# A gated mix of windowed attention and a spatial-gating MLP: row 0's mask by GpSimd fills, softmax maximum and sum by one reduce each, joined last folds, wo scaled one step later, and a PSUM bank of its own for the last 128 output columns

## The chip, the cores and the metric

The kernel runs on one core of a Trainium2 chip. The time is what one execution takes on the device, in microseconds (us). Before the change the median of three runs is 693.05 us (692.97 to 693.73). One further execution was recorded by the hardware profiler; all views of the profile come from it.

A core has five engines that run side by side and wait for each other by semaphores: TensorE (PE, matrix products into PSUM; PEld is its weight load), VectorE (DVE), ScalarE (ACT), GpSimd (POOL) and SyncE (SP, which here only issues DMAs). Each engine takes its instructions in the order in which the program emits them. PSUM has eight banks of 512 fp32 columns on 128 partitions.

## The reference

With S = 2048 rows and D = 1024, cut to what is computed:

```
g   = sigmoid((x * gate_w).sum(-1))                 # one gate per row
a   = attention(x)                                  # 32 heads of 32
        q, k, v = x @ wqkv
        row s attends to rows s, s-2, ..., s-14      # W = 8, dilation 2; negative rows masked
        logits = q . k / sqrt(32); softmax over 8; o = sum of v
        a = o @ wo
b   = gMLP(x)                                       # F = 3584, Fh = 1792
        z = gelu(x @ w_in); z1, z2 = halves; z2 = layernorm(z2)
        b = (z1 * (w_sp @ z2 + b_sp)) @ w_out
out = g * a + (1 - g) * b
```

## The kernel before

All matrix products run on TensorE in one unbroken order: z2's first columns (16 row tiles, L279 to L319), the q, k and v projections in six chunks of 16 tiles (L500 to L519), the rest of z2 (L524), z1 (L576, 14 column tiles of four matmul groups), the two halves of the spatial product as `g_chunk(0)` and `g_chunk(1)` (L593), seven `seven_products` (L701, a Strassen-like scheme for the other half), and last the output products: `mix_pair(0)` (gMLP, rows 0 and 1 of 16 row tiles), `attn_pair(0)` (attention times wo for the same rows) and `both_pairs(q)` for q = 1 to 7.

**Attention** runs on VectorE beside these, for eight groups of four heads. A partition holds 16 consecutive rows. `qk_steps(jh)` (L328) does eight of the 16 rows at a time: one product of q with eight shifted copies of k into `prod`, 8192 elements, then five folds along the head's 32 columns: sums of halves of 16, 8, 4 and 2 columns (all L335, written back into `prod`, where one head's 32 columns take 64 bytes) and the last into the fp32 logits `att_L` (L338). `soft_a` (L342) adds a mask tile, takes the maximum over the window by three halvings and subtracts it; `soft_exp` is one exp on ScalarE; `soft_b` (L352) sums by three halvings, takes the reciprocal and multiplies. `pv_steps(g, jh)` multiplies by v and folds. The logits are laid out as half, window position, row and head, so the eight window positions of one row and head lie 128 bytes apart.

**The order** of the attention's steps between the TensorE work is set by a planner, `Beat` (L220). It keeps a clock of TensorE's columns and one of VectorE; each step comes with a due cost (`4.4`, `2.3` and so on), and after each group of matmuls the planner emits every step that would start within 3 us, and every action whose time (`beat.at`) has come. The costs only set the order of emission. In `attention_steps` (L390) of group g: the folds, `soft_a`, then the two `pv_steps` of group g-1 while exp runs, then `soft_b`. q and k of group g+1 are loaded 1 us (planned) after the folds, v after the `pv_steps`; all these loads and the projections' stores share SP's queue.

**Powers of two.** `whole_power` (L538) finds a scale in steps that are placed apart: a maximum on VectorE, a transpose on TensorE and a reduction on VectorE (L547, L548), a broadcast matmul on TensorE (L550) and the rest on VectorE. For w_out's scale the last two are placed 12 and 24 us after the start of `g_chunk(0)` (L1042). `g_chunk` evacuates each tile on ScalarE (L603), and VectorE adds the bias (L606) and multiplies by z1 (L607), which was stored to DRAM and is loaded back by L460.

**The output.** `mix_pair` (L821) makes seven groups of seven matmuls; the last accumulates into the bank `pb` once VectorE has read it (L842), and the sixth group is read by L844. `wo_scale` (L849) is one VectorE instruction over all of wo in SBUF, which every matmul of `attn_pair` (L893) reads. In `both_pairs` (L905), for the last pair, the last product goes by 384 and 128 columns into one bank, `apb`; each part is combined on VectorE (L883) and stored by SP.

**The mask** tile (L104 to L111) is zero but for row 0's partition, filled with -1e30 where a row has no row to attend to; GpSimd makes it at the start.

Of the kernel before, what the change touches and what calls it, by code (L numbers as in the profile page):

```python
# [15 lines left out]
P = 128  # L16
# [5 lines left out]
HG = 4  # L22
NG = NH // HG
C = HG * DH
W = 8
# [32 lines left out]
def kernel(  # L58
# [42 lines left out]

    ident = sm.tile([P, P], BF, name="ident")
    make_identity(nc, ident[:])
    mask = sm.tile([P, 2 * W * 8 * HG], BF, name="mask")  # L104
    nc.gpsimd.memset(mask[:], 0.0)
    m5 = mask[:].rearrange("p (a w j h) -> p a w j h", a=2, w=W, j=8, h=HG)
    for jh in range(2):
        for w in range(W):
            n = min(8, max(0, 14 - 2 * w - 8 * jh))
            if n > 0:  # L110
                nc.gpsimd.memset(m5[0:1, jh, w, 0:n, :], NEG)  # L111
    zeros = sm.tile([P, NG, 16], BF, name="zeros")
    nc.gpsimd.memset(zeros[:], 0.0)
    g_s = sm.tile([P, 16], F32, name="g_s")
# [30 lines left out]
    v_up = sm.tile([P, 1], I32, name="v_up")  # L145
    back = sm.tile([P, 1], I32, name="back")
    att_L = sm.tile([P, 2 * W * 8 * HG], F32, name="att_L")
    att_m = sm.tile([P, 2, 4, 32], F32, name="att_m")
    att_r = sm.tile([P, 2, 1, 32], F32, name="att_r")
    att_A = sm.tile([P, 2 * W * 8 * HG], BF, name="att_A")  # L150

# [173 lines left out]
    p3 = prod.rearrange("p (w n) -> p w n", w=W)  # L325
    TT = nc.vector.tensor_tensor

    def qk_steps(jh):  # L328
        def mul():
            in0 = _sub_ap(q_t, (8 * jh) * C, [[0, W], [C, 8], [1, C]])  # L330
            in1 = _sub_ap(k_t, (8 * jh) * C, [[2 * C, W], [C, 8], [1, C]])
            TT(prod.rearrange("p (w j c) -> p w j c", w=W, j=8, c=C), in0, in1, ALU.mult)  # L332

        def fold(half):
            return lambda: TT(pv[:, :, 0:half], pv[:, :, 0:half], pv[:, :, half:2 * half], ALU.add)  # L335

        def last():
            TT(L[:, jh * 256:(jh + 1) * 256], pv[:, :, 0], pv[:, :, 1], ALU.add)  # L338

        return [(4.4, mul), (2.3, fold(16)), (1.2, fold(8)), (0.7, fold(4)), (0.6, fold(2)), (0.6, last)]  # L340

    def soft_a():  # L342
        TT(L[:], L[:], mask[:], ALU.add)
        TT(att_m[:], L4[:, :, 0:4, :], L4[:, :, 4:8, :], ALU.max)
        TT(att_m[:, :, 0:2, :], att_m[:, :, 0:2, :], att_m[:, :, 2:4, :], ALU.max)
        TT(att_m[:, :, 0:1, :], att_m[:, :, 0:1, :], att_m[:, :, 1:2, :], ALU.max)
        TT(L4, L4, att_m[:, :, 0:1, :].to_broadcast([P, 2, W, 32]), ALU.subtract)

    def soft_exp():
        nc.scalar.activation(L[:], L[:], ACT.Exp, scale=float(SCALE))  # L350

    def soft_b():  # L352
        TT(att_m[:], L4[:, :, 0:4, :], L4[:, :, 4:8, :], ALU.add)
        TT(att_m[:, :, 0:2, :], att_m[:, :, 0:2, :], att_m[:, :, 2:4, :], ALU.add)
        TT(att_m[:, :, 0:1, :], att_m[:, :, 0:1, :], att_m[:, :, 1:2, :], ALU.add)
        nc.vector.reciprocal(att_r[:], att_m[:, :, 0:1, :])
        TT(A4, L4, att_r[:].to_broadcast([P, 2, W, 32]), ALU.mult)

    def pv_steps(g, jh):
        o_out = obuf[:, :, (g % 2) * C:(g % 2 + 1) * C]  # L360

        def mul():
            in0 = _sub_ap(v_t, (8 * jh) * C, [[2 * C, W], [C, 8], [HG, DH], [1, HG]])
            in1 = _sub_ap(att_A, jh * 256, [[32, W], [HG, 8], [0, DH], [1, HG]])
            TT(prod.rearrange("p (w j d h) -> p w j d h", w=W, j=8, d=DH, h=HG), in0, in1, ALU.mult)  # L365

        def last():
            TT(o_out[:, 8 * jh:8 * jh + 8, :], p3[:, 0, :].rearrange("p (j c) -> p j c", c=C),
               p3[:, 1, :].rearrange("p (j c) -> p j c", c=C), ALU.add)

        return [(4.4, mul), (2.3, lambda: TT(p3[:, 0:4, :], p3[:, 0:4, :], p3[:, 4:8, :], ALU.add)),  # L371
                (1.2, lambda: TT(p3[:, 0:2, :], p3[:, 0:2, :], p3[:, 2:4, :], ALU.add)), (0.7, last)]
# [17 lines left out]
    def attention_steps(t):  # L390
        beat.at(t - 8.0, lambda: load_qk(0))
        beat.at(t + 35.0, lambda: load_v(0))
        for g in range(NG):
            for took, fn in qk_steps(0) + qk_steps(1):
                yield t, took, fn
            t = beat.vector
            if g + 1 < NG:
                beat.at(t + 1.0, lambda g=g: load_qk(g + 1))
            yield t, 2.4, soft_a
            t = beat.vector  # L400
            beat.at(t + (1.0 if g == 0 else 5.0), soft_exp)
            if g == 0:
                t += 5.0
            else:
                for took, fn in pv_steps(g - 1, 0) + pv_steps(g - 1, 1):
                    yield t, took, fn
                t = beat.vector
                if g + 1 < NG:
                    beat.at(t + 1.0, lambda g=g: load_v(g))
                else:  # L410
                    load_v(g)
                if g % 2 == 0:
                    beat.at(t + 1.5, lambda g=g: store_o(g - 1))
            yield t, 2.3, soft_b
            t = beat.vector
        for took, fn in pv_steps(NG - 1, 0) + pv_steps(NG - 1, 1):
            yield t + 5.0, took, fn
        t = beat.vector
        beat.at(t + 14.0, lambda: store_o(NG - 1))
# [398 lines left out]
    def mix_slot(a, n0):  # L818
        return mix_slots[2 * (a % 4) + n0 // 512]
# [85 lines left out]
    def both_pairs(q):  # L905
        a, b = 2 * q, 2 * q + 1
        s, so = row_pair_sums[q % 2], o_sums[q % 2]
        og = [omg[:, r:r + 1] for r in (a, b)]
        ga = [g_s[:, r:r + 1] for r in (a, b)]
        b11, b12, b21, b22 = wo_tiles()  # L910
        a11, a12, a21, a22 = [oT_slots[r % 4][:, 4 * h:4 * h + 4, :] for r in (a, b) for h in range(2)]
        stt = nc.vector.scalar_tensor_tensor
        act = nc.scalar.activation
        wt = [lambda j, k=k: w_t(f_of(q, j), k) for k in range(4)]
        mpa, apa = bank(), bank()
        product7(mpa, u_rows(q, 0, 0), lambda j: w_tiles(f_of(q, j))[0], True)
        mpb = bank()
        nc.scalar.copy(mpb[:], mpa[:])
        product4(apa[:], a11, b11, True)
        apb = bank()  # L920
        nc.scalar.copy(apb[:], apa[:])
        mpe, ape = bank(), bank()
        product7(mpe, s[0], wt[0], True)
        for r in (1, 0):
            act(mix_slot(a + r, 512), mpe[:], ACT.Copy, scale=og[r])
        product4(ape[:], so[0], wo_sums[0], True)
        for r in (1, 0):
            stt(mix_slot(a + r, 512), ape[:], ga[r], mix_slot(a + r, 512), ALU.mult, ALU.add)
        product7(mpb, s[1], wt[1], False)
        mpc, apc = bank(), bank()  # L930
        nc.scalar.copy(mpc[:], mpb[:])
        product4(apb[:], so[1], wo_sums[1], False)
        nc.scalar.copy(apc[:], apb[:])
        product7(mpa, u_rows(q, 0, 1), lambda j: w_tiles(f_of(q, j))[2], False)
        act(mix_slot(a, 0), mpa[:], ACT.Copy, scale=og[0])  # L935
        product4(apa[:], a12, b21, False)
        combine(a, apa[:], 0, 512)
        if a + 4 < 16:
            load_oT(a + 4)
        if q < 7:  # L940
            prepare_o(q + 1)
        if q == 2:
            next(u_steps)
        product7(mpb, s[2], wt[2], False)
        stt(mix_slot(b, 512), mpb[:], og[1], mix_slot(b, 512), ALU.mult, ALU.add)
        product4(apb[:], so[2], wo_sums[2], False)
        combine(b, apb[:], 512, 512)
        product7(mpc, s[3], lambda j: w_tiles(f_of(q, j))[3], False)
        stt(mix_slot(a, 512), mpc[:], og[0], mix_slot(a, 512), ALU.mult, ALU.add)
        product4(apc[:], so[3], b22, False)  # L950
        combine(a, apc[:], 512, 512)
        store_rows_of(a)
        product7(mpb, u_rows(q, 1, 1), wt[3], False)
        act(mix_slot(b, 0), mpb[:], ACT.Copy, scale=og[1])
        if q == 2:
            next(u_steps)
        if q < 7:
            product4(apb[:], a22, wo_sums[3], False)
            combine(b, apb[:], 0, 512)
            store_rows_of(b)  # L960
        else:
            sync.dma_start(out2[b * P:(b + 1) * P, 512:D], ob_slots[b % 4][:, 512:D])
            for n0, nw in ((0, 384), (384, 128)):
                product4(apb[:, n0:n0 + nw], a22, wo_sums[3][:, :, n0:n0 + nw], False)
                combine(b, apb[:, n0:n0 + nw], n0, nw)
                sync.dma_start(out2[b * P:(b + 1) * P, n0:n0 + nw], ob_slots[b % 4][:, n0:n0 + nw])
        if b + 4 < 16:
            load_oT(b + 4)
# [81 lines left out]
    nc.scalar.copy(z2[:, 6, 0:8, :], u_first[:, 0])  # L1050
    u_steps = whole_power(u_up, omg[:, 8:16])
    prepare(1)
    wo_scale()
    mix_pair(0)
    u_sums(6)
    for k in range(4):
        wo_sum(k)
# [38 lines left out]
```

## Time and profile before

| | us |
|---|---|
| median of three runs | 693.05 |
| the profiled execution, its own time | 692.74 |
| its span in the profile | 691.0 |
| TensorE busy | 684.7 |
| VectorE busy | 545.3 |
| ScalarE busy | 386.6 |
| VectorE's first attention step starts | 61.55 |
| last evacuation ends (688.29 + 0.35) | 688.64 |

The TensorE clock is granted in full throughout. In the timeline a line gives start, duration, engine, line of the program, operation, output and input, and in brackets how long the engine sat idle before and what it waited for. In the list of waits a line gives the waiting engine and line, what released it, the total in us, how often, and the longest. In the list of groups a line gives the instructions of one line and shape, their number, and after the bar their busy time in us, the mean duration of one in ns and the idle time before them.

### The profile page before, as it was taken

Reading aid. Unit: us, or ns where it says so; the run is one execution under the profiler, and the core shown is the slowest. Engines: PE = TensorE matmul, PEld = TensorE weight load, DVE = VectorE, ACT = ScalarE, POOL = GpSimd, SP = SyncE. Lnnn points to the kernel's source line nnn. Section 1 sums busy time; section 2 is a strip of 40 time slices with the busy share of each in tenths; the row PEclk is TensorE's granted clock in tenths of the full one; section 3 lists DMA queues with packets and bytes.
Section 4 is the critical chain, followed back from the end, with each engine's and each line's share of the span. In section 5 each row is a group of like instructions: output and inputs, shape, how many; then the busy total and the mean of one; then the engine's idle time right before and its main releaser. Section 6 shows DMA issues by size and latency. Waiting matters only on the chain.

```text
span 691.0 us, 9047 instructions
## 1 busy us (share of the span) xinstructions
PE 684.7 (99%) x3355; PEld 359.9 (52%) x3355; DVE 545.3 (79%) x708; ACT 386.6 (56%) x777; POOL 9.9 (1%) x23
## 2 busy tenths in 40 slices
PE   9999999999999999999999999999999999999997
PEld 4499666666665555444444444444444444444443
DVE  0004889999999999999999999676689988766653
ACT  4345544435478897856775997573665552222332
POOL 1000000000000110000000000000000000000000
PEclk9999999999999999999999999999999999999999
DMA  8995768667665205999877959828111413232210
GB/s 231 187 211 164 167 189 212 151 165 193 182 177 181 88 1 179 195 258 318 307 262 247 280 230 226 229 79 272 34 35 58 152 32 88 64 62 61 74 49 30
DMA packets 186923, 109.19 MB, mean 158 GB/s; under 512 B 145920, under 2 KB 171520, under 8 KB 186624
## 3 DMA queue, kind: packets, MB, share of 16 engines
q1 hardware_dynamic: 184576, 100.23, 54.1%
q10 hardware_dynamic: 2304, 8.39, 3.4%
q8 instruction: 26, 0.43, 0.3%
q14 instruction: 17, 0.14, 0.1%
HBM read 59.77 MB, written 34.67 MB: 137 GB/s over the span
## 4 chain that ended last, share of the span: by engine, by line
PE 95%; DVE 2%; DMA 2%; issue 0%; ACT 0%; DVEq 0%; SPq 0%
PE ps L510 24%; PE ps L288 14%; PE ps L585 14%; PE ps L690 12%; PE ps L816 12%; PE ps L599 11%; PE ps L903 6%; DMA arena<-z_d 1%; PE ps L893 1%; DVE arena L365 1%; DMA z_d<-arena 0%; PE pw L100 0%; DVE arena L335 0%; PE pt L304 0%; PE po L550 0%
## 5 line engine op out<-in xcount | busy, mean ns | idle before, releaser
L510 PE MATMUL ps<-arena 128*128 128x512 bf16 (+1 forms) x896 | 166.2, 349 | 0.0
L510 PEld LDWEIGHTS <-arena 128*128 128x128 bf16 x896 | 120.2, 144 | 45.9
L332 DVE TENSOR_TENSOR arena<-arena 128x8192 bf16<-128x8192 bf16 x16 | 70.8, 4422 | 56.2 <-DMA arena<-k_d 55.9
L513 ACT CAST arena<-ps 128x512 bf16<-128x512 f32 (+1 forms) x112 | 57.7, 527 | 85.1 <-PE ps L510 78.9
L288 PE MATMUL ps<-arena 128*128 128x512 bf16 (+1 forms) x512 | 98.1, 354 | 0.0
L599 PE MATMUL ps<-arena 128*128 128x512 bf16 x448 | 97.7, 379 | 0.0
L585 PE MATMUL ps<-arena 128*128 128x512 bf16 x448 | 96.9, 379 | 0.0
L816 PE MATMUL ps<-arena 128*128 128x512 f16 (+1 forms) x392 | 92.9, 379 | 1.3 <-DVE arena L842 1.3
L690 PE MATMUL ps<-arena 128*128 128x512 bf16 (+1 forms) x392 | 85.5, 379 | 0.0
L335 DVE TENSOR_TENSOR arena<-arena 128x4096 bf16<-128x4096 bf16 (+1 forms) x64 | 77.5, 1212 | 2.0
L288 PEld LDWEIGHTS <-arena 128*128 128x128 bf16 x512 | 50.3, 98 | 47.6 <-issue 1.2
L585 PEld LDWEIGHTS <-arena 128*128 128x128 bf16 x448 | 43.8, 98 | 52.7
L599 PEld LDWEIGHTS <-arena 128*128 128x128 bf16 x448 | 43.4, 98 | 53.0 <-issue 1.4
L365 DVE TENSOR_TENSOR arena<-arena,att_A 128x8192 bf16<-128x8192 bf16 x16 | 70.7, 4421 | 0.3
L816 PEld LDWEIGHTS <-arena 128*128 128x128 f16 (+1 forms) x392 | 38.2, 98 | 47.6 <-issue 1.6
L690 PEld LDWEIGHTS <-arena 128*128 128x128 bf16 (+1 forms) x392 | 38.0, 98 | 45.9 <-issue 0.5
L903 PE MATMUL ps<-arena 128*128 128x512 f16 (+3 forms) x200 | 50.5, 375 | 0.8 <-DVE arena L883 0.8
L293 ACT ACTIVATE arena<-ps 128x512 bf16<-128x512 f32 (+1 forms) x64 | 34.3, 539 | 26.8 <-PE ps L288 26.7
L883 DVE SCALAR_TENSOR_TENSOR arena<-ps,g_s,arena 128x512 bf16<-128x512 f32 (+2 forms) x33 | 24.0, 734 | 29.0 <-ACT arena L935 20.0
L587 ACT ACTIVATE arena<-ps 128x512 bf16<-128x512 f32 x56 | 31.2, 592 | 17.9 <-PE ps L585 14.6
L371 DVE TENSOR_TENSOR arena<-arena 128x4096 bf16<-128x4096 bf16 x16 | 36.6, 2289 | 0.4
L903 PEld LDWEIGHTS <-arena 128*128 128x128 f16 (+1 forms) x200 | 19.4, 98 | 24.1 <-issue 1.2
(170 smaller groups left out, 615.1 us busy)
## 6 DMA issues: line engine op xcount, KB each, us to landing
arena<-k_d SPq DMA_DIRECT2D x8, 960.0 KB
arena<-v_d SPq DMA_DIRECT2D x8, 960.0 KB
z_d<-arena SPq DMA_DIRECT2D x14, 512.0 KB, 4.0
arena<-in_A_wqkv_dram SPq DMA_DIRECT2D x24, 256.0 KB, 4.5
arena<-in_B_w_in_dram SPq DMA_DIRECT2D x4, 1024.0 KB
q_d<-arena SPq DMA_DIRECT2D x32, 128.0 KB, 2.7
k_d<-arena SPq DMA_DIRECT2D x32, 128.0 KB, 2.1
arena<-q_d SPq DMA_DIRECT2D x8, 512.0 KB, 4.6
```

The source lines that it names most:

```text
L288: nc.tensor.matmul(ps[:, 0:N], xT[:, kt, i * P:(i + 1) * P], w2[:, kt, ZC * c:ZC * c + N], start=(kt == 0), stop=(kt == KT - 1))
L332: TT(prod.rearrange("p (w j c) -> p w j c", w=W, j=8, c=C), in0, in1, ALU.mult)
L335: return lambda: TT(pv[:, :, 0:half], pv[:, :, 0:half], pv[:, :, half:2 * half], ALU.add)
L365: TT(prod.rearrange("p (w j d h) -> p w j d h", w=W, j=8, d=DH, h=HG), in0, in1, ALU.mult)
L371: return [(4.4, mul), (2.3, lambda: TT(p3[:, 0:4, :], p3[:, 0:4, :], p3[:, 4:8, :], ALU.add)), (1.2, lambda: TT(p3[:, 0:2, :], p3[:, 0:2, ...
L510: nc.tensor.matmul(ps[:, n0:n1].rearrange("p (t c) -> p t c", c=C), lhsT, wgt[:, pos0:pos1, kt, :], start=(kt == 0), stop=(kt == KT - 1))
L513: nc.scalar.copy(st[:, j % 4, n0:n1], ps[:, n0:n1])
L585: nc.tensor.matmul(ps[:], w1[:, kt, (f % 4) * P:(f % 4 + 1) * P], xT[:, kt, 512 * c:512 * (c + 1)], start=(kt == 0), stop=(kt == KT - 1))
L599: nc.tensor.matmul(ps[:], z2[:, f, i, :], wsp[:, i, :, :].rearrange("p a t -> p (a t)"), start=(i == 0), stop=(i == 15))
L690: nc.tensor.matmul(dst[:], lhs[:, k, :], rhs(k), start=first and k == 0, stop=k == 7, skip_group_check=not first)
L816: nc.tensor.matmul(dst[:], lhs[:, j, :], rhs(j), start=first and j == 0, stop=j == 6, skip_group_check=not first)
L903: nc.tensor.matmul(dst, lhs[:, k, :], rhs[:, k, :], start=first and k == 0, stop=k == 3, skip_group_check=not first)
```

## The change

Five edits:

- The mask tile goes. After the logits of a group are complete, four GpSimd memsets write -1e30 into row 0's partition where the mask stood.
- In `qk_steps` the fold of 4 columns writes into `q_t`, packed as four columns (8 bytes) per logit; the folds of 2 and 1 columns are made once for both halves of the rows, from `q_t` into `q_t` and from `q_t` into `att_L`.
- `soft_a` and `soft_b` take maximum and sum by one `tensor_reduce` over the window each.
- In `attention_steps` `soft_a` comes after the first `pv_steps` of the group before, exp is due 1 us after it in every group, and `soft_b` after the second; the due costs are new.
- `wo_scale` is emitted after `mix_pair(0)`, and for the last pair the last 128 columns get a bank `apd`, into which ScalarE copies their partial sums.

```diff
-    mask = sm.tile([P, 2 * W * 8 * HG], BF, name="mask")
-    nc.gpsimd.memset(mask[:], 0.0)
-    m5 = mask[:].rearrange("p (a w j h) -> p a w j h", a=2, w=W, j=8, h=HG)
-    for jh in range(2):
-        for w in range(W):
-            n = min(8, max(0, 14 - 2 * w - 8 * jh))
-            if n > 0:
-                nc.gpsimd.memset(m5[0:1, jh, w, 0:n, :], NEG)
...
+    q4 = q_t.rearrange("p (n d) -> p n d", d=4)
+    by_window = L4.rearrange("p a w n -> p a n w")
...
-        def last():
-            TT(L[:, jh * 256:(jh + 1) * 256], pv[:, :, 0], pv[:, :, 1], ALU.add)
-
-        return [(4.4, mul), (2.3, fold(16)), (1.2, fold(8)), (0.7, fold(4)), (0.6, fold(2)), (0.6, last)]
+        def to_four():
+            TT(q4[:, 256 * jh:256 * jh + 256, :], pv[:, :, 0:4], pv[:, :, 4:8], ALU.add)
+
+        return [(4.4, mul), (2.3, fold(16)), (1.2, fold(8)), (0.7, to_four)]
+
+    def to_two():
+        TT(q4[:, :, 0:2], q4[:, :, 0:2], q4[:, :, 2:4], ALU.add)
+
+    def to_one():
+        TT(L[:], q4[:, :, 0], q4[:, :, 1], ALU.add)
+        first = L[0:1, :]
+        nc.gpsimd.memset(first[:, 0:128], NEG)
+        for t in range(3):
+            nc.gpsimd.memset(_sub_ap(first, 128 + 32 * t, [[128, 2], [1, 24 - 8 * t]]), NEG)
 
     def soft_a():
-        TT(L[:], L[:], mask[:], ALU.add)
-        TT(att_m[:], L4[:, :, 0:4, :], L4[:, :, 4:8, :], ALU.max)
-        TT(att_m[:, :, 0:2, :], att_m[:, :, 0:2, :], att_m[:, :, 2:4, :], ALU.max)
-        TT(att_m[:, :, 0:1, :], att_m[:, :, 0:1, :], att_m[:, :, 1:2, :], ALU.max)
-        TT(L4, L4, att_m[:, :, 0:1, :].to_broadcast([P, 2, W, 32]), ALU.subtract)
+        nc.vector.tensor_reduce(att_m[:, :, 0, :], by_window, AX.X, ALU.max)
+        TT(L4, L4, att_m[:].to_broadcast([P, 2, W, 32]), ALU.subtract)
 
     def soft_b():
-        TT(att_m[:], L4[:, :, 0:4, :], L4[:, :, 4:8, :], ALU.add)
-        TT(att_m[:, :, 0:2, :], att_m[:, :, 0:2, :], att_m[:, :, 2:4, :], ALU.add)
-        TT(att_m[:, :, 0:1, :], att_m[:, :, 0:1, :], att_m[:, :, 1:2, :], ALU.add)
-        nc.vector.reciprocal(att_r[:], att_m[:, :, 0:1, :])
+        nc.vector.tensor_reduce(att_m[:, :, 0, :], by_window, AX.X, ALU.add)
+        nc.vector.reciprocal(att_r[:], att_m[:])
         TT(A4, L4, att_r[:].to_broadcast([P, 2, W, 32]), ALU.mult)
...
         for g in range(NG):
-            for took, fn in qk_steps(0) + qk_steps(1):
+            for took, fn in qk_steps(0) + qk_steps(1) + [(1.2, to_two), (1.1, to_one)]:
                 yield t, took, fn
             t = beat.vector
             if g + 1 < NG:
                 beat.at(t + 1.0, lambda g=g: load_qk(g + 1))
-            yield t, 2.4, soft_a
+            if g == 0:
+                t += 3.0
+            else:
+                for took, fn in pv_steps(g - 1, 0):
+                    yield t, took, fn
+                t = beat.vector
+            yield t, 1.4, soft_a
             t = beat.vector
-            beat.at(t + (1.0 if g == 0 else 5.0), soft_exp)
+            beat.at(t + 1.0, soft_exp)
             if g == 0:
                 t += 5.0
             else:
-                for took, fn in pv_steps(g - 1, 0) + pv_steps(g - 1, 1):
+                for took, fn in pv_steps(g - 1, 1):
                     yield t, took, fn
...
-            yield t, 2.3, soft_b
+            yield t, 2.0, soft_b
...
+        if q == 7:
+            apd = bank()
+            nc.scalar.copy(apd[:, 384:512], apb[:, 384:512])
         product4(apc[:], so[3], b22, False)
...
-            for n0, nw in ((0, 384), (384, 128)):
-                product4(apb[:, n0:n0 + nw], a22, wo_sums[3][:, :, n0:n0 + nw], False)
-                combine(b, apb[:, n0:n0 + nw], n0, nw)
+            for ps, n0, nw in ((apb, 0, 384), (apd, 384, 128)):
+                product4(ps[:, n0:n0 + nw], a22, wo_sums[3][:, :, n0:n0 + nw], False)
+                combine(b, ps[:, n0:n0 + nw], n0, nw)
                 sync.dma_start(out2[b * P:(b + 1) * P, n0:n0 + nw], ob_slots[b % 4][:, n0:n0 + nw])
...
     prepare(1)
+    mix_pair(0)
     wo_scale()
-    mix_pair(0)
     u_sums(6)
```

More of the change, by code (lines that the diff above doesn't have):

```diff
@@ L147 @@
     att_L = sm.tile([P, 2 * W * 8 * HG], F32, name="att_L")
-    att_m = sm.tile([P, 2, 4, 32], F32, name="att_m")
+    att_m = sm.tile([P, 2, 1, 32], F32, name="att_m")
     att_r = sm.tile([P, 2, 1, 32], F32, name="att_r")
```

## The prediction

> **What bounds the kernel now.** I read the page first: the share of each engine, then the idle times of the costliest groups. TensorE is the bound; VectorE has a fifth of the span free, so a shorter VectorE instruction gains nothing unless TensorE waits for it.
>
> ```profile
> PE 684.7 (99%) x3355; PEld 359.9 (52%) x3355; DVE 545.3 (79%) x708; ACT 386.6 (56%) x777; POOL 9.9 (1%) x23
> ```
>
> Then TensorE's waits. These three are all of it after the start, and the change touches all three: L816, L903 and L550 stand behind the places that it edits or reorders.
>
> ```profile
> PE ps L816 <- DVE arena L842: 1.3, 1, 1.3
> PE ps L903 <- DVE arena L883: 0.8, 1, 0.8
> PE po L550 <- DVE top L548: 0.7, 1, 0.7
> ```
>
> Third, the timeline around each wait. At 391 us TensorE needs the reduction L548, which stands in VectorE's queue behind attention work and the gated chunk's first tiles. That queue was itself held at 378.25 until the load of z1 from DRAM had come (1.27 us idle): an anchor that no VectorE saving moves.
>
> ```profile
> 376.56 0.42 DVE L606 TENSOR_TENSOR arena<-arena 128x512 bf16<-128x512 bf16 x1
> 378.25 0.42 DVE L607 TENSOR_TENSOR arena<-arena 128x512 bf16<-128x512 bf16 x1 [1.27 <-DMA arena<-z_d]
> ...
> 390.94 0.27 DVE L548 TENSOR_REDUCE top<-po 1x1 bf16<-1x128 bf16 x1
> ...
> 391.27 0.37 PE L550 MATMUL po<-top,const-bfloat16-1.0 1*128 1x512 bf16 x1 [0.68 <-DVE top L548]
> ```
>
> Around the first mixer pair: wo's scaling (L850) stands ahead of L842, for which TensorE waits.
>
> ```profile
> 558.66 2.35 DVE L850 TENSOR_SCALAR arena<-arena,wo_up 128x8192 bf16<-128x8192 bf16 x1
> 560.92 0.74 DVE L842 SCALAR_TENSOR_TENSOR arena<-ps,omg,arena 128x512 f32<-128x512 f32 x1
> 561.58 0.74 DVE L844 SCALAR_TENSOR_TENSOR arena<-ps,omg,arena 128x512 f32<-128x512 f32 x1
> 561.72 1.67 PE L816 MATMUL ps<-arena 128*128 128x512 f16 x7 [1.33 <-DVE arena L842]
> ```
>
> And the end: the last four 128-column matmuls wait for the evacuation of the 384 columns beside them.
>
> ```profile
> 687.20 0.62 DVE L883 SCALAR_TENSOR_TENSOR arena<-ps,g_s,arena 128x384 bf16<-128x384 f32 x1 [1.48 <-ACT arena L954]
> 687.87 0.38 PE L903 MATMUL ps<-arena 128*128 128x128 f16 x4 [0.78 <-DVE arena L883]
> 688.29 0.35 DVE L883 SCALAR_TENSOR_TENSOR arena<-ps,g_s,arena 128x128 bf16<-128x128 f32 x1 [0.47 <-PE ps L903]
> ```
>
> Last, the groups by shape, for the prices. L335's halves of 2048 and 1024 take 1.223 and 0.694 us (0.157 fixed, 0.52 ns an element); fp32 at 512 takes 0.692 (0.157 and 1.04 ns). Two rows break the pattern: their elements lie 64 bytes apart.
>
> ```profile
> L335 DVE TENSOR_TENSOR arena<-arena 128x512 bf16<-128x512 bf16 x16 | 10.2, 640 | 0.5
> L338 DVE TENSOR_TENSOR att_L<-arena 128x256 f32<-128x256 bf16 x16 | 9.8, 614 | 0.6
> L343 DVE TENSOR_TENSOR att_L<-att_L,mask 128x512 f32<-128x512 f32 x8 | 5.5, 692 | 0.3
> L277 ACT COPY arena<-arena 128x1024 bf16<-128x1024 bf16 x8 | 15.7, 2005 | 0.0
> ```
>
> Less the 0.157, L338 pays 1.79 ns an element and the 512 form of L335 1.89 ns a pair. ScalarE's L277 also reads 64 bytes apart: 2.0 us, against 1.05 for a dense copy of 1024 (L1050).
>
> **The change, part by part.** (1) *Tail.* The 128 columns get their own bank, so their matmuls follow the 384 at once: 686.28 + 4 x 0.16 + 0.38 = 687.30. VectorE is busy with the 384 until 687.82 and then takes 0.35: 688.17, and SP, which issued the first store at 687.85 and needs some 0.38 per issue, issues the second at 688.23, not at 688.67. That is -0.4 us (0 if the first store's landing sets the end, no more than 0.44). The added copy into the new bank goes to ScalarE, idle from 680 to 686.5 there (L954 waits 6.4 us): nothing; without that cover, about 0.4 (L513's 256-column form takes 0.38).
>
> (2) *wo scaled later.* L842 no longer waits for L850: the fifth of the six products that start at 551.15, at 0.216 a matmul, ends at 558.87, so L842 is done by 559.65 and TensorE goes on at 560.23 instead of 561.72. But every matmul of the attention pair reads the scaled wo. L844 needs the sixth product, which ends at 560.38, and runs 560.42 to 561.16; L850 follows from 561.08 (two neighbours overlap by 0.08) for 2.35 to 563.43, and TensorE's L893 starts at 563.49. It started at 563.22 before. The stall changes place: +0.27. Behind L850 stand wo's four sums and the first two evacuations, which have eight banks of cover.
>
> (3) *Attention on VectorE*, off TensorE's path except through L548. Per group before: 2 x (0.640 + 0.614) for the last two folds, 2.33 for L343 to L347, 2.18 for L353 to L357. After: two joined folds (1024 and 512 outputs, chunks 8 bytes apart), a reduce and L347's subtract (0.692), a reduce, the reciprocal (0.553) and the product (0.693). No row shows a strided reduce. Its elements lie 128 bytes apart, so it lies between 0.69 (dense fp32, 512 elements) and 512 x 1.79 ns + 0.157 = 1.07; I take 1.07, since L338 is the row nearest in stride. For the joined folds the ends are 0.69 each (512 cycles, dense) and 1.12 and 1.07 (every pair or element pays as at 64 bytes), for the first even 1.22 (one element a cycle). I take 0.69: the 1024 form of L335 reads 8-byte chunks at the full dense rate. [...]
>
> When does VectorE reach the first L606? Before at 376.56; it may be at 377.80 without delaying L607. The planner's arithmetic, with its new due costs, gives the new order: all of group 7's folds and group 6's first probability product now come before it, where before it stopped after the second fold of group 7's second half. And exp of group 0 is issued one projection tile later: cast 87.8 to 88.4, table load 1.28, exp 0.63, so the first normalising starts at 90.34 instead of 88.64: +1.7. From there (0.035 less for each instruction that falls away): seven second reduces 7 x (1.07 - 0.936 - 0.07) = +0.5; six first ones 6 x (1.07 - 1.634 - 0.10) = -4.0; six groups' folds 6 x (1.38 - 2.508 - 0.07) = -7.2; group 7 1.25 + 0.73 + 1.46 - 1.32 + 4.45 = +6.6. Sum -2.4: 374.1, in time by 3.7. VectorE only waits longer for z1.
>
> From L607 to L548, 5.7 us fall out (folds and softmax of group 7) and 2.32 + 1.26 + 0.70 (product sums), 1.07 and 0.69 come in: +0.35, or -0.03 with reduces of 0.69. So L550's wait grows from 0.7 to about 1.0.
>
> (4) *Waits and queues.* The q load now waits for the second joined fold, as it overwrites q. On SP the k load and the q, k, v or z1 stores queue behind it: in the order as worked through 1 us at folds of 0.69, 6 us in the late case below. They have two or three stage slots of 6.9 us, then eight banks of 1.7 us: 0, or, if the cover went, that wait. exp is issued 1 instead of 5 us after its subtract, and ScalarE's evacuations queue behind it, 1 us up to group 6, and 6 us in group 7, where each of the eight banks lasts 3.5: nothing again. The row-0 fills are four short GpSimd memsets a group (L111's took 0.107, L113's 0.195: at most 0.8), hidden behind four VectorE instructions of 8.7 us; uncovered they would eat the 3.7 and cost 2. GpSimd's L438 (1 to 3 us) can stand ahead of them, also inside 8.7. Dropping the mask empties GpSimd's first 2 us, where the first transposes wait for x by DMA: nothing. The later v loads move about 14 us earlier, with their VectorE work: nothing. Attention ends about 10 us earlier, and nobody waits: TensorE shows no wait between 392 and 560.
>
> Sum: -0.40 + 0.27 + 0.35 = +0.2 us. The profiled execution took 692.74 (span 691.0 and 1.74 around it), 0.31 under the median 693.05, so 692.97 there and **693.3** against the median: no change.
>
> **Rivals.** *Late queue (slower).* The joined folds pay 1.12 and 1.07 a group, as the diff's due costs of 1.2 and 1.1 also suggest. Then folds are 6 x (2.19 - 2.578) = -2.3 and group 7 +7.4: VectorE reaches L606 at 379.8, 2.0 too late, and L548, L550 and all of TensorE with it: 693.3 + 2.0 = 695.3; with 1.22, 696.0. It decides from an arrival of 377.8, which is 1.9 us for both folds at reduces of 1.07. Against it: with the due costs taken whole (they leave 0.7 for a reduce) VectorE arrives at 375.7, and the time is 692.9.
>
> *Hidden scaling (faster).* If L850 ended before the last product of the pair, at 561.7, the 1.49 of L842's stall would be gained: -1.49 - 0.40 + 0.35 = -1.5, 691.5. It would have to start by 559.4, but L844 stands before it and needs the sixth product.
>
> *The tail does nothing*: the first store lands last. 693.7, within no change.
>
> **How the numbers follow.** No change, with or without the tail: 0.58. Late queue 0.30 and another stall of the kind in (4) 0.03: slower 0.33. Hidden scaling or a larger gain of that kind: faster 0.09. A change of 0.2% (1.4 us) is about what a measurement of this kernel can tell from none. The likeliest case alone spans 692.6 to 693.9 (its ends: reduces of 0.69, no gain in the tail). Range: 692.2, leaving out most of the faster case, to 696.2, which takes in the late queue at its dearest.
>
> **What would show it.** L816's wait for L842 gone and a wait of about 1.7 before L893 for L850; no wait in the last L903; reduces at 1.07; the joined folds at 0.69 each; L607 still starting at 378.2 after a longer DMA wait; L550 waiting about 1. It is wrong if L607 starts after 378.3, if L893 does not wait, or if TensorE waits anywhere between 62 and 366 us.

## The result and the profile after

The changed kernel takes **702.5 us** (median of four runs, 701.54 to 702.86) against 693.01 of the kernel before beside it: a ratio of 1.0134, 95% interval 1.0117 to 1.0152. It is slower by 1.3%, and 6.3 us beyond the upper end of the range given. Its profiled execution took 702.48 with a span of 700.4, 9.4 more than before. Lines of the changed kernel's z1, g and output stages stand 6 to 9 higher than before: L587 is now L593, L607 is L613, L548 is L554, L550 is L556, L816 is L822, L850 is L856, L893 is L899.

The page's first part and its row of the clock: VectorE has 14 us less to do, and the clock, full throughout before, has a dip in the slice at 385 to 402 us.

```profile
PE 683.9 (98%) x3307; PEld 360.3 (51%) x3355; DVE 531.5 (76%) x652; ACT 385.8 (55%) x778; POOL 13.7 (2%) x44
...
PEclk9999999999999999999999799999999999999999
```

TensorE's longest waits (engine, line, what released it, total, number, longest). The first was 0.7 before; the second is the wait that was forecast.

```profile
PE po L556 <- DVE top L554: 7.1, 1, 7.1
PE ps L899 <- ACT arena L852: 1.7, 1, 1.7
```

The timeline around the first. VectorE arrives at the gated chunk at 372.53, 1.6 us earlier than forecast, and then stands still for 11.69 us: the load of z1 ends 6.39 us later than before (384.64 against 378.25). From there to the reduction it takes 12.84 us, against 12.69 before.

```profile
372.53 0.42 DVE L612 TENSOR_TENSOR arena<-arena 128x512 bf16<-128x512 bf16 x1
384.64 0.42 DVE L613 TENSOR_TENSOR arena<-arena 128x512 bf16<-128x512 bf16 x1 [11.69 <-DMA arena<-z_d]
...
397.48 0.27 DVE L554 TENSOR_REDUCE top<-po 1x1 bf16<-1x128 bf16 x1
...
397.81 0.58 PE L556 MATMUL po<-top,const-bfloat16-1.0 1*128 1x512 bf16 x1 [7.14 <-DVE top L554]
```

Windows of TensorE after it (stretch, length, busy time and number, granted clock, DMA share, GB/s): half clock from about 393.6 to 403.8, partly while it waits and partly once it works again.

```profile
390.00:394.00 4.00, 0.67 (x4) 0.95 1.07 218
394.00:398.00 4.00, 0.19 (x1) 0.50 1.06 368
398.00:402.00 4.00, 4.00 (x10) 0.50 0.97 405
402.00:406.00 4.00, 4.00 (x16) 0.77 0.93 372
```

So the 9.4 us are: L556 starts 6.54 later (397.81 against 391.27); from L556 to the first mixer matmul it takes 162.8 instead of 159.9, +2.9, the half clock; from there to the attention matmuls of the mixer (L899) 12.45 instead of 12.07, +0.4; the end -0.43.

**Why z1 is late.** z1 is stored tile by tile by SyncE, from two staging slots, and the load behind L613 needs the last store. SyncE's queue before (L589 here is the twelfth store of z1, L379 a load of v, L383 the store of o):

```profile
351.45 0.46 SPq L566 DMA_DIRECT2D arena<-in_A_wo_dram  x1
352.94 0.36 SPq L589 DMA_DIRECT2D z_d<-arena  x1
353.39 0.46 SPq L379 DMA_DIRECT2D arena<-v_d  x1
357.70 0.64 SPq L383 DMA_DIRECT2D o_d<-arena  x1
...
369.63 0.33 SPq L460 DMA_DIRECT2D arena<-z_d  x1
```

and after. The later v load and `store_o(5)`, which writes 1 MB in 2048 pieces of 512 bytes, now stand ahead of the last look load (L572, the end of a pass over w_out and wo that sums |w| for their scales; L566 before) and of the twelfth store of z1 (the second L595 here). The look load takes 4.98 us to issue, and the twelfth store goes out at 358.51 instead of 352.94.

```profile
351.44 0.37 SPq L595 DMA_DIRECT2D z_d<-arena  x1
351.87 0.50 SPq L379 DMA_DIRECT2D arena<-v_d  x1
...
352.46 0.92 SPq L383 DMA_DIRECT2D o_d<-arena  x1
353.48 4.98 SPq L572 DMA_DIRECT2D arena<-in_A_wo_dram  x1
...
358.51 0.52 SPq L595 DMA_DIRECT2D z_d<-arena  x1
...
376.51 0.33 SPq L466 DMA_DIRECT2D arena<-z_d  x1
```

ScalarE shows what that does to the gelus (L593): one waits 4.39 us for its slot. Behind it stand sums of |o| (L386, 0.82 us each with its read-out), which belong to the same store and were all behind the last gelu before. The last gelu starts at 370.77. Before (the first view) it started at 365.99.

```profile
365.99 0.60 ACT L587 ACTIVATE arena<-ps 128x512 bf16<-128x512 f32 x1 [1.13 <-PE ps L585]
```

```profile
364.82 0.60 ACT L593 ACTIVATE arena<-ps 128x512 bf16<-128x512 f32 x1 [4.39 <-DMA z_d<-arena]
...
369.05 0.63 ACT L386 ACTIVATE arena<-arena 128x512 bf16<-128x512 bf16 x1
...
370.77 0.58 ACT L593 ACTIVATE arena<-ps 128x512 bf16<-128x512 f32 x1
```

The 6.39 us follow: last gelu +4.78; from it to the issue of the load 5.74 instead of 3.64, +2.10; from there to L613 8.13 instead of 8.62, -0.49. The 2.10 is the landing of the last store (issued at 371.37, before at 366.61). Probably it is slower because it now meets a load by ScalarE's queue (L621, issued at 370.91; before at 369.66, when that store had landed): from 370.8 to 376.5 us that queue moves 0.93 MB beside the store's 0.52 MB. No run tries this by itself. TensorE itself finished z1 at the same time, 365.96 against 365.88 before: its banks covered the late gelus, as the prediction had it. What it did not cover was the load behind them.

The small terms, in the list of groups by shape (after the bar: busy time, mean ns of one, idle before). Joined folds and strided reduces have the prices taken:

```profile
L348 DVE TENSOR_REDUCE att_m<-att_L 128x64 f32<-128x512 f32 x8 | 8.4, 1046 | 0.5 <-POOL att_L L345 0.5
L338 DVE TENSOR_TENSOR arena<-arena 128x1024 bf16<-128x1024 bf16 x8 | 5.5, 693 | 0.3
L341 DVE TENSOR_TENSOR att_L<-arena 128x512 f32<-128x512 bf16 x8 | 5.5, 692 | 0.3
```

The mixer pair and the end, in the timeline: the wait stands before L899, with wo's scaling (L856) ending at 572.95 just ahead of it; and the eight matmuls of 384 and 128 columns run in one block.

```profile
570.61 2.34 DVE L856 TENSOR_SCALAR arena<-arena,wo_up 128x8192 bf16<-128x8192 bf16 x1
...
573.05 3.18 PE L899 MATMUL ps<-arena 128*128 128x512 bf16 x14 [1.72 <-ACT arena L852]
...
696.11 1.04 PE L909 MATMUL ps<-arena 128*128 128x384 f16 x8
...
697.67 0.81 SPq L975 DMA_DIRECT2D out_dram<-arena  x2
```

### The profile page after: what moved, and what is told of

It is laid out like the page before. It is cut to its first block, busy times and chain, and to the rows that moved or that the text cites. A ratio compares the mean times of both kernels' runs of the same rounds, so it can differ in the third digit from the quotient of the medians.

```text
span 700.4 us, 8978 instructions
## 1 busy us (share of the span) xinstructions
PE 683.9 (98%) x3307; PEld 360.3 (51%) x3355; DVE 531.5 (76%) x652; ACT 385.8 (55%) x778; POOL 13.7 (2%) x44
## 4 chain that ended last, share of the span: by engine, by line
PE 81%; DMA 8%; ACT 4%; SPq 3%; DVE 2%; issue 2%; DVEq 0%; ACTq 0%
PE ps L516 24%; PE ps L280 14%; PE ps L696 12%; PE ps L822 12%; PE ps L605 11%; PE ps L909 6%; DMA z_d<-arena 4%; DMA arena<-in_B_w_out_dram 2%; PE ps L591 2%; SPq L463 2%; ACT arena L593 1%; ACT arena L574 1%; DMA arena<-z_d 1%; PE ps L899 1%; SPq L572 1%
## 5 line engine op out<-in xcount | busy, mean ns | idle before, releaser
L516 PE MATMUL ps<-arena 128*128 128x512 bf16 (+1 forms) x896 | 166.2, 349 | 0.0
L280 PE MATMUL ps<-arena 128*128 128x512 bf16 (+1 forms) x501 | 97.0, 352 | 1.4 <-DMA arena<-in_B_w_in_dram 0.7
L822 PE MATMUL ps<-arena 128*128 128x512 f16 (+1 forms) x380 | 91.2, 379 | 0.5
L696 PE MATMUL ps<-arena 128*128 128x512 f16 (+1 forms) x385 | 84.7, 379 | 0.6 <-issue 0.3
L822 PEld LDWEIGHTS <-arena 128*128 128x128 f16 (+1 forms) x392 | 38.3, 98 | 46.1
L330 DVE TENSOR_TENSOR arena<-arena 128x4096 bf16<-128x4096 bf16 (+1 forms) x32 | 56.2, 1757 | 1.0
L593 ACT ACTIVATE arena<-ps 128x512 bf16<-128x512 f32 x56 | 31.2, 595 | 25.5 <-DMA z_d<-arena 12.6
```

Of the source, the lines that this page charges most:

```text
L280: nc.tensor.matmul(ps[:, 0:N], xT[:, kt, i * P:(i + 1) * P], w2[:, kt, ZC * c:ZC * c + N], start=(kt == 0), stop=(kt == KT - 1))
L516: nc.tensor.matmul(ps[:, n0:n1].rearrange("p (t c) -> p t c", c=C), lhsT, wgt[:, pos0:pos1, kt, :], start=(kt == 0), stop=(kt == KT - 1))
L593: nc.scalar.activation(z1s[:, c, :], ps[:], ACT.Gelu_apprx_tanh)
L696: nc.tensor.matmul(dst[:], lhs[:, k, :], rhs(k), start=first and k == 0, stop=k == 7, skip_group_check=not first)
L822: nc.tensor.matmul(dst[:], lhs[:, j, :], rhs(j), start=first and j == 0, stop=j == 6, skip_group_check=not first)
```

## The experiments

Theory after the result: the place of `store_o(5)` and of its sums costs all of it, by way of z1, and the long stall then costs clock. Rivals: the new VectorE instructions or the GpSimd fills cost time themselves; TensorE's place for the broadcast is at fault; only the transfers, or only the sums, matter.

**e1: the store one tile later, and its sums with it.** Nothing else of the change is undone.

```diff
-                    beat.at(t + 1.5, lambda g=g: store_o(g - 1))
+                    beat.at(t + (8.0 if g == 6 else 1.5), lambda g=g: store_o(g - 1))
```

> The changed kernel, with the store of attention groups 4 and 5 to DRAM issued behind the twelfth of the fourteen z1 stores on SP's queue, instead of ahead of it and of a load of wo; the eight absolute sums on ScalarE that hang on that store move back with it. Theory A (the reordered SP queue holds the twelfth z1 store, ScalarE then waits for its staging slot, the last z1 store and the reload of z1 are late, and TensorE waits for the broadcast): the twelfth z1 store is issued at about 353 instead of 358.5 us, L613 starts at 378 to 379.5 instead of 384.6, the wait before L556 falls from 7.1 to 0.7 to 2, the granted clock stays at 1.0, and the time is 692.9 to 694.5. Rival B (the eight absolute sums on ScalarE, placed among z1's last evacuations, are the cause): the same time, told apart by the next run. Rival C (VectorE itself, GpSimd fills or reduces are the cause): no change, 702.5.

693.12 us, ratio 1.0001 (0.9992 to 1.0010). The whole loss is gone. L613 stands where it stood before, and the wait for the load is what the earlier arrival makes of it:

```profile
372.49 0.42 DVE L612 TENSOR_TENSOR arena<-arena 128x512 bf16<-128x512 bf16 x1
378.15 0.43 DVE L613 TENSOR_TENSOR arena<-arena 128x512 bf16<-128x512 bf16 x1 [5.24 <-DMA arena<-z_d]
```

L556 waits 0.67, the clock is full (1.0), L899 still waits 1.72. The later v load still stands ahead of the twelfth store of z1 here (351.49 against 353.07), as in the change: moving it alone costs nothing that can be measured. So the other edits together move nothing that can be measured.

**e2: the sums alone later.** The transfers keep the order of the change; the eight sums come 14 us later, behind the last gelu.

```diff
-        lag = 1.0 if g + 1 == NG else 12.0
+        lag = 1.0 if g + 1 == NG else 26.0 if g == 5 else 12.0
```

> The changed kernel, with only the eight absolute sums of that store moved 14 us later on ScalarE; SP's queue is as in the changed kernel. Theory A: the twelfth z1 store stays at 358.5 and ScalarE still waits 4.4 us for its slot; the last evacuation comes some 2 us earlier because three sums no longer stand before it, L613 at about 382.6, the wait before L556 about 5, the time 699.5 to 701. Rival B: 692.9 to 694.5. Rival C: 702.5.

698.63 (698.46 to 700.23), ratio 1.0087 (1.0072 to 1.0102): 5.8 over before, a little less than expected. The gelu waits as long as in the changed kernel; the load of z1 is issued at 371.07, L556 waits 4.59, and half clock follows, for 6.8 us.

```profile
364.08 0.60 ACT L593 ACTIVATE arena<-ps 128x512 bf16<-128x512 f32 x1 [4.10 <-DMA z_d<-arena]
```

The 5.8 is not the price of the transfers alone. Moved so far, the sums stand behind the fold (L368) that writes group 6's first part into the buffer that they read (the first of them read it in place of group 4's). ScalarE waits for it, and VectorE in its turn for an evacuation (L609) behind the first sum:

```profile
386.26 0.63 ACT L386 ACTIVATE arena<-arena 128x512 bf16<-128x512 bf16 x1 [12.32 <-DVE arena L368]
...
387.49 0.43 DVE L612 TENSOR_TENSOR arena<-arena 128x512 bf16<-128x512 bf16 x1 [1.26 <-ACT arena L609]
```

From L613 (380.87) to L554 it takes 14.23 us, 1.4 more than in the change.

**e3: the broadcast 12 us later.** TensorE is to ask for the reduction when it is there.

```diff
-        beat.at(t0 + 12.0 + 12.0 * k, lambda: next(w_steps))
+        beat.at(t0 + 12.0 + 24.0 * k, lambda: next(w_steps))
```

> The changed kernel, with the broadcast matmul of w_out's scale (L556) placed 36 instead of 24 us after the start of the first spatial product; everything up to it is as in the changed kernel, so z1 is as late. Theory A says that the late z1 costs only through this one wait and the clock that falls after it: no wait before L556, granted clock 1.0, 702.5 - 7.1 - 3.1 = 692.3 (692.0 to 692.9). If the lateness of z1 and of VectorE's queue cost anywhere else, 694 to 700.

695.76 (693.34 to 699.08), ratio 1.0047 (1.0029 to 1.0066): a miss. There is no wait left before L556, but VectorE is still late when TensorE comes to wo's maximum, 28 us further on, where before there was no wait; and three idle microseconds there again bring half clock, for 3.4 us.

```profile
432.04 0.27 PE L553 MATMUL po<-ident,top_b 128*1 128x128 bf16 x1 [2.99 <-DVE top_b L549]
```

The lateness belongs to VectorE's queue, and to no one place at which TensorE asks.

**e4: a pure delay in the kernel before.** Fourteen needless VectorE instructions of 0.46 us ahead of L548.

```diff
+        if up1 is w_up:
+            for _ in range(14):
+                TT(waste[:], waste[:], waste[:], ALU.max)
         v.tensor_reduce(top_1[:], pt, AX.X, ALU.max)
```

> The kernel before, with 14 needless VectorE instructions (256 fp32 each, 0.46 us from start to start) ahead of L548, so that the broadcast matmul waits 6.4 us longer and nothing else is touched. If the stall and the clock are the whole of the loss: a wait of about 7.1, the granted clock below 1.0 in the 16 us around it, and 693.0 + 6.4 + 3.1 = 702.5. If the clock fell for another reason than the stall: 699.4.

701.5, ratio 1.0127 (1.0110 to 1.0144). A late reduction by itself, with z1 on time, gives nearly the whole loss: its matmul waits 6.43, and from there to the mixer it takes 161.4, 1.5 more than before. The stall grew by 5.75 where 6.4 was expected, and the clock's part is half of the 3.1. Of the 8.5 us that the span of the profiled execution is longer than before, 1.2 have nothing to do with the delay: z1 already ends at 367.11 there, against 365.88, after a longer wait for w_in at the start.

**e6: the sums alone early.** The store later as in e1, its sums left where the change has them.

```diff
-        lag = 1.0 if g + 1 == NG else 12.0
+        lag = 1.0 if g + 1 == NG else 5.5 if g == 5 else 12.0
...
+                    beat.at(t + (8.0 if g == 6 else 1.5), lambda g=g: store_o(g - 1))
```

> The store of o's group 5 is issued after the twelfth store of z1, as before the change, but its eight sums on ScalarE stand where the change has put them, five of them (0.82 us each) among the last gelus. Theory (the issue that SyncE holds behind the 2048-piece store costs the larger part, and the sums cost only because the gelus had already lost 4.4 us to the missing slot): the twelfth store is issued at about 353, L593 waits for no slot, the eight banks of TensorE take up the sums, the load of z1 ends by 380.5 and L613 starts at 378.2 to 380.5; time 693 to 695. Rival (the sums alone delay the last store of z1 by 4 us): L613 at 382 or later, L556 waits 4 to 5 us, the granted clock falls again; time 697 to 699.

697.66 (695.75 to 699.55), ratio 1.0074 (1.0056 to 1.0091). My theory that the sums cost nothing on their own fell; the rival holds, though L613 and the wait stay just short of its figures. One gelu waits 1.89 us for its slot, where none was expected; in e1 one waits 1.47, and there it does no harm. The last gelu starts at 369.04, the load is issued at 372.87, and in the profiled execution, the slowest of the four:

```profile
381.80 0.43 DVE L613 TENSOR_TENSOR arena<-arena 128x512 bf16<-128x512 bf16 x1 [8.25 <-DMA arena<-z_d]
...
394.99 0.58 PE L556 MATMUL po<-top,const-bfloat16-1.0 1*128 1x512 bf16 x1 [3.69 <-DVE top L554]
```

**e7: the look load ahead of the store.** The transfer behind the 2048 pieces is then the twelfth store of z1.

```diff
-        beat.at(beat.now + 3.0 + 8.0 * k, lambda src=src, slot=slot: sync.dma_start(
+        beat.at(beat.now + 3.0 + 8.0 * k - (6.5 if k == 10 else 0.0), lambda src=src, slot=slot: sync.dma_start(
```

> The order of the change, but the last load of the look over the weights is issued ahead of the store of o's group 5 and not behind it. So the transfer behind the 2048-piece store is the twelfth store of z1. Theory (SyncE is held for about 5 us at whatever transfer stands behind the store of 2048 pieces): the twelfth store is the one held, is issued at about 358 to 359 again, the load of z1 ends at 384 or later, and the time is 701 to 703. Rival (the look's load itself takes 5 us to issue there): the hold goes ahead of the store, the time depends on where it ends; if it is not held at all when it stands ahead, the twelfth store goes out at 354 and the time is 694 to 698, the sums among the gelus being what is left.

702.77, ratio 1.0146 (1.0125 to 1.0166), as the theory had it. Now it is this issue that takes five microseconds and more, although it came early:

```profile
353.84 5.73 SPq L595 DMA_DIRECT2D z_d<-arena  x1
```

**e8: the store by another queue.** As e2, with `store_o(5)` issued by ScalarE.

```diff
-        sync.dma_start(dst, obuf)
+        (nc.scalar if g == 5 else sync).dma_start(dst, obuf)
```

> As e2 (the order of the change, with the sums 14 us later), but the store of o's group 5 is issued by ScalarE and not by SyncE. Theory (it is SyncE's issuing that is held behind 2048 pieces): the last look load and the twelfth store of z1 go out at 352 to 354, L593 waits under 2 us for a slot, L613 at 378.2 to 380; time 692.5 to 694.5. Rival (the 2048 pieces hold up the DMA engines, whoever issues them): the twelfth store goes out early but lands as late as before, at 363 to 365, L593 waits about 4 us for its slot as in e2, L613 at 380.5 or later; time 697 to 699.

698.28 (697.24 to 699.56), ratio 1.0088 (1.0071 to 1.0104): the rival by the time and by the gelu's wait. (L613, at 379.32, falls into the theory's range; the time is long all the same, as VectorE waits 1.26 us for L609 as in e2 and takes 14.24 us from L613 to L554.) ScalarE issues o's store at 348.06, where SyncE did at 351.94 in e2. SyncE is no longer held, and the twelfth store goes out at 353.87, 4 us earlier than in e2; but it lands at the same time, 363.9 in e8 (10.0 us after its issue) and 364.0 in e2 (6.1 after), and the gelu waits as in e2.

```profile
352.69 1.13 SPq L572 DMA_DIRECT2D arena<-in_A_wo_dram  x1
353.87 0.54 SPq L595 DMA_DIRECT2D z_d<-arena  x1
...
364.01 0.60 ACT L593 ACTIVATE arena<-ps 128x512 bf16<-128x512 f32 x1 [4.30 <-DMA z_d<-arena]
```

So the held issue is a sign and not the cause: issued at 353.84 to 358.51, the twelfth store lands at 363.9 to 364.7 in all four runs that have o's store ahead of it (e8, e7, e2, the change). From 350 to 362 us the DMA engines of e8 are busy throughout (0.85 to 1.08 in windows of two microseconds, 262 to 375 GB/s). In the changed kernel 2.5 MB of v, o and wo stand between the eleventh store of z1 and the twelfth, which at some 300 GB/s are about 8.5 us; that this sum sets the landing is worked out, not tried by itself. In e8 o's store, issued on ScalarE's queue ahead of v's load, the look load and both stores of z1 on SyncE's, lands 14.2 us after its issue (10.6 in e1, where it stands on SyncE's queue). From 351 to 362 us ScalarE's queue moves 0.67 MB and SyncE's 2.82 MB, so the two went on side by side.

**e12: the change with the planner's old figures.** The instructions of the change, all of them; only the two planned durations of the softmax steps are those of before.

```diff
-            yield t, 1.4, soft_a
+            yield t, 2.4, soft_a
...
-            yield t, 2.0, soft_b
+            yield t, 2.3, soft_b
```

> All instructions of the change, but the planner is told the durations of before for the two softmax steps (2.4 and 2.3 us where the change says 1.4 and 2.0). It then writes the orders of before at this place by itself: the last look load and the twelfth store of z1 ahead of the later v load and the store of o's group 5, and all eight sums behind the last gelu. Theory (what costs is the place of that store and of its sums, not an instruction of the change): L613 at 377.9 to 378.6, L556 waits 0.5 to 1.2 us, no half clock; time 692.3 to 693.7. Rival (the new instructions or the GpSimd fills themselves cost time): above 695.

692.82, ratio 1.0015 (0.9993 to 1.0037). The planner puts the later v load and the store back behind the twelfth store of z1, and the time is that of before. L613 starts at 380.45, 2 us later than expected, but fewer attention steps then stand between it and L554, and L556 does not wait at all. The twelfth store goes out at 357.19 here, nearly as late as in the change (358.51), but with v's load and o's store behind it the gelu at 361.22 finds its slot free. One of the ten runs took 700.37, which has no explanation here.

The runs about the place of the store, in us against the kernel before beside each:

| | o's store behind the 12th z1 store | o's store ahead of it |
|---|---|---|
| sums behind the last gelu | e1 +0.3, e12 +0.2 | e2 +5.8, e8 +5.7 |
| sums among the last gelus | e6 +5.1 | the change +9.5, e7 +10.3 |

Only the store ahead, or only the sums early, shows a loss of over 5, both together 9.5: they act on the same gelus. The entries of e2 and e8 hold the 1.4 us between L613 and L554 that moving the sums brought in. Read by the issue of the load of z1 (369.63 before, 369.65 in e1), the store's place alone makes it 1.4 us late (371.07 in e2, 371.03 in e8), the sums alone 3.2 (372.87 in e6, 0.7 of it a later end of z1 on TensorE), both 6.9 (376.51). Without the 1.4 the stall would be some 3.2 us in e2 and 1.9 in e8, worked out from their 4.59 and 3.32; no run shows whether one of 1.9 costs clock, so what the store's place alone costs in time stays open.

**e5: half the delay of e4,** seven instructions in place of 14.

> The kernel before with seven needless VectorE instructions of 0.46 us ahead of the reduction L548: L550's wait grows from 0.7 to 3.9 us. Theory (a stall costs its own length, and from about 3 us on also half clock for whole steps of 3.4 us, of which half of what lies behind the restart is lost): 3.2 of the stall and 1 to 3 of the clock; time 696.9 to 699. Rival (the clock falls only in stalls of over 4 us): 695.8 to 696.4, the clock full throughout.

698.2, ratio 1.0080 (1.0065 to 1.0095), as expected. The wait is 3.61 and still costs clock, 161.6 in place of 159.9 up to the mixer. The one-microsecond windows show that it falls at 395.6, when TensorE is back at work since 394.38:

```profile
394.00:395.00 1.00, 0.62 (x3) 1.00 0.90 387
395.00:396.00 1.00, 1.00 (x6) 0.81 1.03 430
396.00:397.00 1.00, 1.00 (x4) 0.50 1.05 449
```

**e9 and e10: both kernels mended.** e9 is the change with the store later (e1), the broadcast 4 us later, and wo's scaling in two halves of 512 columns, one right behind the first combination of the pair (L848), the other behind the last. e10 is the kernel before, attention and mask untouched, with the same broadcast and halves and the change's bank for the last columns.

```diff
+        wo_scale(0)
...
-    def wo_scale():
-        nc.vector.tensor_scalar(wo_sb, wo_sb, wo_up[:].bitcast(F32), None, ALU.mult)
+    def wo_scale(h):
+        half = wo_sb[:, :, 512 * h:512 * h + 512]
+        nc.vector.tensor_scalar(half, half, wo_up[:].bitcast(F32), None, ALU.mult)
...
-        beat.at(t0 + 12.0 + 12.0 * k, lambda: next(w_steps))
+        beat.at(t0 + 12.0 + 16.0 * k, lambda: next(w_steps))
```

> The changed kernel with the store of o's group 5 and its sums issued one tile later, the broadcast of the look's maximum 4 us later, and the scaling of wo in two halves of 512 columns, the first one behind the first combination of the mixer pair, the second behind the last. Theory: the three stalls of TensorE are gone or short. Against 692.85 before: -0.43 of the tail, -0.7 at the broadcast, and -0.6 to -1.3 of the 1.7 before the attention matmuls; time 690.4 to 691.5. Rival (the vector engine is late for the broadcast wherever it stands, or the halves of the scaling come in the way of the combination): 692.5 to 694.

> The kernel before, with its attention on VectorE as it was, and the same repairs: the last 128 columns in a bank of their own, the broadcast 4 us later, the scaling of wo in halves. Theory (the edits in attention give TensorE nothing, so both mended kernels are equal): 690.4 to 691.5, within 0.2% of the mended changed kernel. Rival (the 14 us that VectorE saves in attention matter once the stalls are gone): at least 1 us slower than the mended changed kernel.

690.36, ratio 0.9969 (0.9958 to 0.9980), and 690.32, ratio 0.9967 (0.9954 to 0.9979): both beat both kernels. They gain 2.2 us of the 2.4 that two waits of before (1.33 at L816, 0.68 at L550) and the tail (0.43) add up to. What is left of TensorE's waits in e9:

```profile
PE pw L100 <- PEq L1091: 0.8, 1, 0.8
PE ps L280 <- DMA arena<-in_B_w_in_dram: 0.6, 1, 0.6
PE ps L696 <- issue: 0.3, 2, 0.2
```

That the two are equal is the answer on the attention edits: 14 us less on VectorE (531.6 against 545.4 busy) are worth nothing to TensorE.

## Why the prediction was wrong, and where it was right

**The step that failed** is the anchor. The third view says that VectorE's queue was held until the load of z1 had come, "an anchor that no VectorE saving moves". The load hangs on the last store of z1, this on ScalarE's gelus, these on staging slots that earlier stores must free; and those stores share SyncE's queue and the DMA engines with transfers that the planner places by VectorE's clock. I followed the anchor downstream only. It moved by 6.39 us.

**Its entry in the sum** is in part (4): "The later v loads move about 14 us earlier, with their VectorE work: nothing." For the v loads this held: e1 keeps the later one ahead of the twelfth store and loses nothing. But the list stopped at them. The store of o's group 5, which `attention_steps` emits 0.5 us after the v load, and the eight ScalarE sums that the store brings with it are not named at all. Left at nothing, their move measured +9.5. Part (4) did weigh late stores of z1, behind a q load, but asked only whether slots and banks cover TensorE ("0, or, if the cover went, that wait"), not when the load of z1 comes that needs the last of them. The profile of before had the warning: from 356 to 364 us, around the thirteenth store of z1 (issued at 359.76), its DMA engines are busy at 0.98 to 1.13 of their time.

**The clock** was not in the sum, and is 2.9 of it.

**The terms that were priced** came close. Reduces 1.046 (1.07 taken); joined folds 0.693 and 0.692 (0.69 taken), so the late queue, my slower rival, does not exist: VectorE reached the gated chunk at 372.53, earlier than the 374.1 forecast, and the time is lost in another way. That it is the stride which a reduce pays for is not shown by itself, as no run has a dense reduce of that size. From L613 to L554 +0.15 (+0.35). The mixer: no wait before the pair's last product, 1.72 before L899 (1.7), +0.38 up to it (+0.27); hidden scaling did not happen. The tail 4.29 instead of 4.72 from the 384-column matmuls to the end, -0.43 (-0.40). The fills take 0.91 us a group (at most 0.8 taken) and cost VectorE 0.5 us in all. e1, with that one store and its sums moved back, is 0.3 us over the kernel before beside it, where +0.2 was forecast for the whole change; its interval cannot tell either from zero.

**The chances**: slower had 0.33, but 0.30 of it for a mechanism that did not happen and 0.03 for "another stall of the kind in (4)", which did. The sign "it is wrong if L607 starts after 378.3" was the right one.

## What to carry to other kernels

When a change moves a planned order, list everything that the moved steps emit, stores and follow-up work on other engines included, and look at the stage in which each lands: what its queue, the DMA engines and the receiving engine are doing there. A wait called an anchor is to be followed upstream to what sets it, and a schedule written from planned durations is changed by the figures alone (e12), so that a faster instruction can cost more than it saves. Before VectorE is relieved, the waits of the bounding engine say what that can be worth: here two waits and the tail, 2.4 us, of which the kernel before takes 2.2 without it (e10).

## What was not expected of the hardware

**Half clock lasted 3.4 us, or two or three times that.** From the granted clock of the windows, half clock (0.50) lasted 10.2 us in the changed kernel (wait 7.14) and in e7 (9.81), 6.8 in e4 (6.43), e2 (4.59) and e6 (3.69), and 3.4 in e5 (3.61), e8 (3.32) and e3 (2.99): one, two or three times 3.4 in these eight runs. It began 2.6 (e6) to 4.9 us (e5) after TensorE had become idle. Half of what lay behind the restart was lost, 1.5 to 3.1 us. The stall of 2.99 in e3 so cost some 4.6, and that of 0.7 before, with the clock granted in full, cost only itself. What sets these lengths and the moment of the fall is not shown: in e6 and e3 the clock fell after 2.6 and 2.8 us of idleness, in e5 4.9 us after its start, when TensorE was back at work.

**A store of 1 MB in 2048 pieces** took between 5.7 us (before) and 14.2 (e8) to land, and the DMA issued right behind it on its queue took 4.85, 4.98 and 5.73 us to issue (a look load in e2 and the change, a store of z1 in e7), instead of about 0.4. The one behind it in the kernel before, issued 2 us later, took 1.40.
